# A fused attention and feed-forward kernel: table loads and filler products as operations of their own, in a new written-out order

## The chip, the cores and the metric

The kernel runs on one core of one Trainium2 chip. The metric is the device time of one execution in microseconds. Five engines work beside each other, each through its own queue in order: PE (TensorE, matrix products), ACT (ScalarE, table functions and scaling), DVE (VectorE), POOL (GpSimd) and SP (SyncE, which here only issues DMA).

## The reference, cut to what matters

```python
# q, k, v: (4, 8, 768, 64), proj: (64, 6); w_in: (512, 2048), w_out: (2048, 512)
q_bits = (np.einsum('bhsd,dk->bhsk', q, proj) > 0)       # the same for k
q_bucket = np.sum(q_bits * 2 ** np.arange(6), axis=-1)
mask = q_bucket[:, :, :, None] == k_bucket[:, :, None, :]
scores = np.where(mask, q @ k.T / 8, -1e9)
attn = softmax(scores)                                   # over the last axis, + 1e-9
x = (attn @ v).transpose(0, 2, 1, 3).reshape(3072, 512)
h = x @ w_in
out = (h * tanh(softplus(h))) @ w_out                    # Mish
```

Attention is allowed only between a query and a key whose six sign bits agree; the result, of 3072 rows, goes through a feed-forward block with the Mish function.

## The kernel before

The work is cut into units of 256 query rows (two chunks of 128) over all eight heads: 12 units, three to each of the four batches. A unit has eight **slots** of attention (four pairs of heads, two chunks), numbered n = 0 to 95 over the kernel, and eight **groups** m of the feed-forward block (256 of the 2048 inner columns each), 0 to 95 as well, which run some slots behind.

Most fp32 values are carried as the sum of two fp16 numbers (hi and lo), so that PE can work in fp16: each long product is three fp16 products. Unit 0 is the exception: its probabilities are transposed on PE in fp32 and its products are fp32, since the weights have not been split yet.

A slot n is made of these operations, named as in the code: `S{n}` scores on PE (L878), `max` over the keys on DVE (L884), `scl` two or four small DVE or POOL instructions that make the scale and bias of the exponential (L890 to L896), `exp` two on ACT (L909), `sums` and `rv` (L922 to L931) the reciprocal of the row sums. In unit 0, `tp32` transposes the probabilities on PE (L950) and `tc32` copies them back (L955); later units form `hi` and `lo` (L374, L375, L390) and transpose through DMA (`ptturn`). `V{p}` is the product with V (L992, L999). `H{m}` is the first feed-forward product (L1044 to L1050), `mish` its function on ACT (L1066), `g_hi` and `g_lo` its split, `O{m}` the second product (L1095 to L1101).

Unit 0 carries one-time work as well: the K, Q and V of the first batch are scaled by the size of their squares (`square` on ACT or `gram` on PE, L438, with `trace` on DVE, L440, then `st` on PE, L457 and L458, `half` and `pw`), split (`k_hi`, `k_lo`, ...), transposed (`tp` on PE, L414, `tc`, or through DMA) and hashed (`hp` on PE, L712, `hsum` and `bits` on DVE, L716 and L720). The weights are converted (`w_u`, `w_sign` L543, `w_low` L556 or L559, `w_join` L563) and later split (`w_hi`, `w_lo`).

ACT holds one table of functions at a time. Exp and Mish are in different tables; scaling, copying and squaring are in both. Before the change the loads (ACT_TABLE_LOAD) are placed by the compiler ahead of the first function that needs the other table.

**What sets the order.** Every operation is recorded by `op(name, alternatives, reads, writes)`, with one alternative for each engine that could do it and a cost in ns. `ORDER` is a table of numbers, worked out ahead by a planner that is not part of the file: it gives the operations in the order in which they are issued, a letter behind a number picking the second, third or fourth alternative (another engine). So each engine's queue, and which engine does a step, follow from this table. The functions that the change touches are `gram`, `att_front`, `att_exp` and `ffn_mish`.

Of the kernel before, what the change touches and what calls it, by code (L numbers as in the profile page):

```python
# [14 lines left out]
AF = mybir.ActivationFunctionType  # L15
# [3 lines left out]
P = 128  # L19
# [68 lines left out]
37 88 14 22 7 0 3 1 2 23 24 25 63 73 38c 6 8 9 13 10 15 152 5 4 40 41 18 19 42 74 11b 12 20 21 26c 53b 75 76 77b 43 28  # L88
39b 29 66 16 44 55 30 45 27c 46 47 48 307 54 31 32 65 78 34 79 49 33 35 36b 67 83 84 213 214 215 89 90b 50 62 51 56 52
80 81 82 114b 91 168 169 85 86 113 87 153b 104 108 109 110b 17 92 93 94 123 57 58 59 60 115c 154b 95 96 97 170 99 98  # L90
100 111 105 112 132 101 102 155 69 70 162c 116 64 133 171 124b 172 61 103 135 136 68 256 257 258 129d 130 137 117 134
147 156 173b 148 149 138 139 140 141 72 107 131 118 119 120 106 121 144 145 150 163b 175 157 151 158 159 160 142 146
71 205b 164 165 464 185 125c 186 188 189 190 174b 126 143b 211 212 206b 207 216b 122 187 200 201 176 167 177 178 180
202 166 191 192 197 198 308 309 372 378 193b 373 374 179 208 458 459 460 194 182d 183 199 225 203 379 128 380 184 127
204 226 248 375 227 222 223 249b 250c 251 254 230b 161 231 376c 229 228 310b 224 240 241 242 232c 233 243 244 245 311b
247 195 268 269 270 246 219c 305 271 209 265 272 196b 210 273 217 253 274b 266 255 461b 236d 237 238 262d 263 465 181
283 284 234 220 275 286 276 267 279c 285 259b 287 221 239 466 235 260 370 293c 292 294 295b 264 252 299 280 281 277
288 289 291 261 290 313c 300 301b 278 326b 462b 296 297 218b 282b 314 306 315 371 321 322 323c 324 312 327 328b 317
325 298 318 316c 432 434 329 330 344d 302 303 352 467 433 456 319 320 345 353 354 304 332b 333 435 347c 346 348 349
463 483 350 351 355 457 484 356 391 334c 335 336 337 468b 357 383b 384 385 441 485 486 392 393 338c 394 387 487 488  # L100
# [103 lines left out]
KV0 = (-1, -0.5, 0, 2)  # L204
WAT = (0, 2, 4, 5, 6, 7, 8, 8, 9, 9, 9, 11, 11, 11, 11, 11)
Q_AT = 2
SECOND = (1, 3, 5, 7)
QPE, KPE = 4, 2
KV_GRAM, Q_GRAM = 4, 2
LAG = 3  # L210


def BACKBONE(NA, NM):


    for blk in range(NA // 4 + LAG):
# [1038 lines left out]
```

## Time and profile before

| what | value |
|---|---|
| median of 3 runs | 843.06 us (841.53 to 843.43) |
| the profiled execution, its own time | 841.4 us |
| its span from first to last instruction | 839.6 us |
| PE busy | 794.9 us (95%) |
| DVE busy | 714.6 us (85%) |
| ACT busy | 632.1 us (75%), of which 92 table loads |
| POOL busy | 93.6 us (11%) |
| table loads ahead of Exp, ahead of Mish | 45 of 1283 ns, 46 of 1283 ns |

The profiled execution is 1.66 us under the median. The shares are means over very different stages: the first 182 us hold unit 0 and the one-time work, and PE, DVE and ACT take turns; after that PE is busy nearly without a break. An instruction's idle time is the time in which its engine had nothing else to do before it, and the releaser is what ended that. "PEclk" is the share of the full clock that TensorE was granted; half of it is 1.2 GHz.

### The profile page before, as it was taken

What the parts mean: (1) busy time and instruction counts of PE and PEld (TensorE: products, weight loads), DVE (VectorE), ACT (ScalarE), POOL (GpSimd) and SP (SyncE); (2) the same over time, 40 slices, a digit from 0 to 9 for tenths busy, and PEclk for the clock granted to TensorE, in tenths of its full rate; (3) what the DMA queues carried; (4) which work ended last, traced back from release to release, by engine and by line L of the source; (5) the groups of instructions that cost most, each with busy time, mean ns of one, the idle gap of its engine ahead of it and who ended that gap; (6) DMA issues with size and microseconds to landing.
All of it is one profiled execution on the core that took longest, in us unless ns stands there. A gap on an engine that the chain in (4) does not pass through costs nothing. (4 is left out here: it accounts for less than half of the span.)

```text
span 839.6 us, 16631 instructions
## 1 busy us (share of the span) xinstructions
PE 794.9 (95%) x6508; PEld 546.2 (65%) x6508; DVE 714.6 (85%) x1334; ACT 632.1 (75%) x972; POOL 93.6 (11%) x96
## 2 busy tenths in 40 slices
PE   4788989789999999999999999999999999999997
PEld 4656556466668578578577586577577577576664
DVE  6798999898989888989998998899999889888522
ACT  6777889987798687689878688679888688587410
POOL 5445424322230000000000000000000000000000
PEclk9899999999999999999999999999999999999999
DMA  9985878769999869899989987899997848655700
GB/s 281 197 253 178 215 179 195 120 147 186 203 181 181 165 120 158 175 171 180 185 170 175 159 176 154 142 171 196 201 157 159 168 96 160 123 95 102 157 1 26
DMA packets 400303, 135.58 MB, mean 161 GB/s; under 512 B 370528, under 2 KB 391008, under 8 KB 400224
## 3 DMA queue, kind: packets, MB, share of 16 engines
q1 hardware_dynamic: 400224, 134.52, 80.3%
q8 instruction: 51, 0.84, 0.4%
q14 instruction: 28, 0.23, 0.1%
HBM read 35.65 MB, written 6.29 MB: 50 GB/s over the span
## 5 line engine op out<-in xcount | busy, mean ns | idle before, releaser
L909 ACT ACTIVATE pb<-ps_s,svb 128x768 f32<-128x768 f32 x192 | 188.7, 986 | 58.6 <-DVE svb L896 50.6
L1048 PE MATMUL ps_acc<-X,wi 128*128 128x256 f16 x704 | 191.9, 273 | 0.8 <-ACT ffb L1066 0.8
L1050 PE MATMUL ps_acc<-X,wi 128*128 128x256 f16 x704 | 191.8, 273 | 0.0
L1049 PE MATMUL ps_acc<-X,wi 128*128 128x256 f16 x704 | 191.8, 272 | 0.0
L884 DVE TENSOR_REDUCE svb<-ps_s 128x2 f32<-128x1536 f32 x96 | 168.2, 1752 | 14.7 <-PE ps_s L878 11.1
L390 DVE SCALAR_TENSOR_TENSOR hl<-pb,svb,hl 128x768 f16<-128x768 f32 x172 | 174.5, 1022 | 6.5 <-ACT hl L374 4.0
L878 PE MATMUL ps_s<-KT,QT 128*128 128x512 f16 (+1 forms) x768 | 141.8, 328 | 6.3 <-ACT pb L909 5.3
L1099 PE MATMUL ps_o<-wo,ffb 128*128 128x512 f16 x352 | 133.4, 379 | 0.0
L1101 PE MATMUL ps_o<-wo,ffb 128*128 128x512 f16 x352 | 133.4, 379 | 0.0
L1100 PE MATMUL ps_o<-wo,ffb 128*128 128x512 f16 x352 | 133.4, 379 | 0.0
L878 PEld LDWEIGHTS <-QT 128*128 128x128 f16 x768 | 73.3, 98 | 56.6 <-issue 14.5
L374 ACT ACTIVATE hl<-pb,svb 128x768 f16<-128x768 f32 x80 | 73.4, 930 | 35.0 <-DMA PT<-hl 21.4
L992 PE MATMUL ps_t<-PT,VT 128*64 128x256 f16 x1584 | 94.6, 274 | 3.0 <-DMA PT<-hl 2.3
L1066 ACT ACTIVATE ffb<-ps_acc,smalls 128x512 f32<-128x512 f32 x88 | 59.3, 684 | 48.0 <-PE ps_acc L1050 46.9
L992 PEld LDWEIGHTS <-VT 128*64 128x64 f16 x1584 | 83.8, 110 | 17.3 <-issue 16.8
L1049 PEld LDWEIGHTS <-wi 128*128 128x128 f16 x704 | 68.8, 98 | 12.9 <-issue 1.8
L1048 PEld LDWEIGHTS <-wi 128*128 128x128 f16 x704 | 68.8, 98 | 11.6 <-issue 1.6
L1050 PEld LDWEIGHTS <-wi 128*128 128x128 f16 x704 | 68.8, 98 | 8.3 <-issue 0.2
L390 DVE SCALAR_TENSOR_TENSOR ffb<-ffb,smalls 128x512 f16<-128x512 f32 x88 | 65.2, 747 | 3.4 <-ACT ffb L374 0.9
L909 ACT ACT_TABLE_LOAD x45 | 57.7, 1283 | 12.1 <-DVE svb L896 4.7
L1101 PEld LDWEIGHTS <-ffb 128*128 128x128 f16 x352 | 34.4, 98 | 41.5
L1066 ACT ACT_TABLE_LOAD x46 | 59.0, 1283 | 0.8
(212 smaller groups left out, 991.9 us busy)
## 6 DMA issues: line engine op xcount, KB each, us to landing
out_dram<-ffb SPq DMA_DIRECT2D x24, 256.0 KB, 2.8
stg<-in_q_dram SPq DMA_DIRECT2D x10, 512.0 KB, 4.8
stg<-in_k_dram SPq DMA_DIRECT2D x12, 384.0 KB, 3.9
stg<-in_v_dram SPq DMA_DIRECT2D x12, 384.0 KB, 3.6
wo<-in_moe_w_out_dram SPq DMA_DIRECT2D x7, 512.0 KB, 4.9
stg<-in_moe_w_out_dram SPq DMA_DIRECT2D x7, 512.0 KB, 4.4
stg<-in_moe_w_in_dram SPq DMA_DIRECT2D x6, 512.0 KB, 4.5
wi<-in_moe_w_in_dram SPq DMA_DIRECT2D x6, 512.0 KB, 4.5
```

What stands on the lines that cost most here:

```text
L390: return [("DVE", 215 + 1.035 * n, port(lambda: nc.vector.scalar_tensor_tensor(out=dst, in0=src, scalar=sc, in1=hi, op0=ALU.mult, op1=ALU. ...
L878: nc.tensor.matmul(sc[:, hh * S + c0 * P:hh * S + c1 * P], QTb[:, u % 2, sl, qi], KTb[:, j, sl, hh * NCH + c0:hh * NCH + c1].rearrange("p ...
L884: op("max", [("DVE", 1790, lambda: nc.vector.tensor_reduce(out=sv[:, 0], in_=sc.rearrange("p (h e) -> p h e", h=2), axis=AX.X, op=ALU.max, ...
L909: EXP[n, hh] = op("exp", [("ACT", 1075, lambda hh=hh, t=t: nc.scalar.activation(pb[:, t], sc[:, hh * S:(hh + 1) * S], AF.Exp, bias=sv[:, 2 ...
L992: nc.tensor.matmul(pv[hh * D:(hh + 1) * D, 0:256], vt[:, w, hh * NCH + c], pt[:, hh, a * NCH + c].rearrange("p s t -> p (s t)"), start=(x ...
L1048: nc.tensor.matmul(o, wh, X[:, 0, c], start=(c == 0), stop=False)
L1049: nc.tensor.matmul(o, wh, X[:, 1, c], start=False, stop=False)
L1050: nc.tensor.matmul(o, wl, X[:, 0, c], start=False, stop=(c == NCC - 1))
L1066: op("mish", [("ACT", 690, lambda: nc.scalar.activation(ffb[:, t], PS[psn], AF.Mish, scale=h))], [psn] + ([(hsn, g, g + 1)] if u else []), ...
L1099: nc.tensor.matmul(PS[f"o{s}"], gh, hi[:, e], start=first, stop=False)
L1100: nc.tensor.matmul(PS[f"o{s}"], gh, lo[:, e], start=False, stop=False)
L1101: nc.tensor.matmul(PS[f"o{s}"], gl, hi[:, e], start=False, stop=last)
```

## The change

Three things are added as operations, and `ORDER` is a new table from a planner in which two rules of waiting were corrected (the planner's text is not part of the kernel).

- `fill`: ahead of each of the eight slots of unit 0, four operations that each issue eight 128x128x128 products of ones into an unused part of the PSUM bank `ps_g`; each has an empty alternative. The new table takes 10 of the 32: two ahead of the first PE operation, two behind the first two `st`, two among the first transposes, two between the scores of slots 0 and 1, and two behind the scores of slot 2. The other 22 are empty.
- `pre_e` and `pre_m`: ahead of each pair of `exp` and each `mish`, an operation that loads the table, with an empty alternative. The new table takes 12 of 96 and 7 of 96. Where none is taken, the compiler still places its own load. The program then has 94 loads besides the first one (before: 91); one of the 7 is followed by a second load of the same table.
- `gram` had two places in `ps_g`, used in turn; it now has one, since `fill` takes the second.

```diff
@@ the first and the last line of the table @@
-37 88 14 22 7 0 3 1 2 23 24 25 63 73 38c 6 8 9 13 10 15 152 5 4 40 41 18 19 42 74 11b 12 20 21 26c 53b 75 76 77b 43 28
...
+2967 2968 2961c 2962 2969 2914 2911 2970b 2971b 2972 2973 2974b 2975b 2976
@@ above BACKBONE @@
+NFILL = 4
@@ gram @@
-        i = 2 * half + gram_n[half] % 2
-        gram_n[half] += 1
+        i = 0
@@ att_front @@
+        if u == 0:
+            for _ in range(NFILL):
+                def busy():
+                    for _ in range(8):
+                        nc.tensor.matmul(ps_g[:, P:2 * P], ones, ones, start=True, stop=True)
+                BANK.append(op("fill", [("PE", 427, busy), ("PE", 0, lambda: None)], ["ones"]))
         op(f"S{n}", [("PE", 1300, pe)], [(f"QT{u % 2}.{x}", 4 * j, 4 * j + 4) for x in range(2)] +
@@ att_exp @@
+        op("pre_e", [("ACT", 1290, lambda: nc.scalar.preload_act_table(AF.Exp)), ("ACT", 0, lambda: None)])
@@ ffn_mish @@
+        op("pre_m", [("ACT", 1290, lambda: nc.scalar.preload_act_table(AF.Mish)), ("ACT", 0, lambda: None)])
```

Where the new table leads differs from the old one from the start to about the place that PE reached at 373 us before, DVE at 387 us and ACT at 384 us; behind that the queues of PE, DVE and ACT hold the same operations in the same order. Line numbers of the changed file are 11 to 19 higher: L884 is L901, L720 is L731, L1066 is L1085.

On PE, the first `gram` now stands behind the first transposes (it stood between the first two `st`); the second keeps its place among the hashes ahead of the last transposes of the K of slot 0, but the load that it reads (K of the third pair of heads) is issued seventh and no longer ninth; the third stands behind those transposes (it stood among them), ahead of the last `st` and of S0; and the fourth behind S0. On SP the first weights' load goes from the eighth place to the fifteenth.

The queue of DVE behind the maximum of slot 0 (svb holds the softmax numbers of a slot, hsum and hsum_k the sums of the hash, tok_65 and PT take the hash bits, ps_g is the bank of `gram`). Before:

```order
L884 TENSOR_REDUCE svb<-ps_s 128x2
L890 TENSOR_SCALAR svb<-svb,smalls 128x1 x2
L894 TENSOR_SCALAR svb<-svb 128x1 x2
L716 TENSOR_REDUCE hsum<-ps_t 128x72
L720 TENSOR_SCALAR tok_65<-hsum 128x12x6 x2
L384 COPY PT<-PT 128x12x64
L716 TENSOR_REDUCE hsum_k<-ps_t 128x72
L720 TENSOR_SCALAR PT<-hsum_k 128x12x6 x2
L850 TENSOR_SCALAR smalls<-smalls 128x1
```

After:

```order
L901 TENSOR_REDUCE svb<-ps_s 128x2
L451 SCALAR_TENSOR_TENSOR ps_g,smalls<-ps_g,ffb 128x128
L727 TENSOR_REDUCE hsum<-ps_t 128x72
L731 TENSOR_SCALAR tok_65<-hsum 128x12x6
L861 TENSOR_SCALAR smalls<-smalls 128x1
L727 TENSOR_REDUCE hsum_k<-ps_t 128x72
L731 TENSOR_SCALAR PT<-hsum_k 128x12x6 x2
L861 TENSOR_SCALAR smalls<-smalls 128x1
L472 TENSOR_SCALAR smalls<-ps_t 128x1
L396 COPY wo<-wo 128x12x64
L731 TENSOR_SCALAR tok_65<-hsum 128x12x6
```

The four instructions of the scale of slot 0 (L890, L894) are gone from DVE, `trace` has come in, and the first of the two bits of tok_65 and the bits of hsum_k stand ahead of the second.

POOL at the same place (L548 is `w_sign`, L925 `sums`, L372 a hi part; in the changed file L559, L943, L384). Before:

```order
L372 TENSOR_SCALAR stg<-stg 128x1024
L381 TENSOR_SCALAR wo<-wo 128x12x64
L548 TENSOR_SCALAR wi<-stg 128x1024
L925 TENSOR_SCALAR svb<-svb 128x2
L548 TENSOR_SCALAR wo<-wo 128x1024
L552 TENSOR_SCALAR wo<-wo 128x1024
```

After:

```order
L384 TENSOR_SCALAR wo<-wo,smalls 128x12x64
L907 TENSOR_SCALAR svb<-svb,smalls 128x2
L913 TENSOR_TENSOR svb<-svb 128x2
L384 TENSOR_SCALAR PT<-X,smalls 128x12x64
L457 TENSOR_SCALAR smalls<-smalls 128x1
L820 TENSOR_SCALAR smalls<-smalls 128x1
L559 TENSOR_SCALAR wo<-wo 128x1024
L943 TENSOR_SCALAR svb<-svb 128x2
```

The scale of slot 0 (L907, L913) is now on POOL between two hi parts of K, and the `w_sign` that stood ahead of the sums has moved back. In the same way the scales of slots 11, 13 and 14 and, later, 19 have come to POOL; slot 9's has gone from it to DVE.

ACT around the Mish of group 5 (wi and wo are weights being split or converted, tok_64 takes the hi part of Q). Before:

```order
L424 ACTIVATE wo,smalls<-wo 128x1024
L1066 ACT_TABLE_LOAD
L1066 ACTIVATE ffb<-ps_acc_820 128x512
L374 ACTIVATE tok_64<-X,smalls 128x16x64
L424 ACTIVATE wi,smalls<-wi 128x1024
L909 ACT_TABLE_LOAD
L909 ACTIVATE pb,svb<-ps_s,svb 128x768
```

After:

```order
L386 ACTIVATE wo<-wo,smalls 128x1024
L1084 ACT_TABLE_LOAD
L567 ACTIVATE wo<-wo 128x512
L436 ACTIVATE wo,smalls<-wo 128x1024
L1085 ACTIVATE ffb<-ps_acc_896 128x512
L386 ACTIVATE tok_64<-X,smalls 128x16x64
L924 ACT_TABLE_LOAD
L927 ACTIVATE pb,svb<-ps_s,svb 128x768 x2
```

The load for Mish (L1084, an operation of its own) stands two steps ahead of the function, and the load for Exp (L924) stays right ahead of it.

## Rows read from the trace of the kernel before

**Rows 1.** Windows by stage: busy us (instructions) of each engine, granted clock, DMA share, GB/s.

```profile
0.00:42.00 42.00, 27.10 (x260) 22.14 (x262) 29.20 (x82) 29.70 (x45) 21.57 (x27) 0.92 0.94 239
42.00:182.00 140.00, 118.49 (x765) 78.37 (x760) 130.82 (x224) 120.31 (x177) 52.23 (x50) 0.98 0.74 182
182.00:347.00 165.00, 164.53 (x1408) 114.00 (x1408) 146.70 (x280) 132.08 (x207) 19.82 (x20) 1.00 0.94 174
347.00:780.00 433.00, 429.42 (x3680) 295.91 (x3679) 387.98 (x718) 337.28 (x526) 0.00 (x0) 1.00 0.85 157
```

**Rows 2.** Groups by line within 42 to 182 us: busy, mean ns, idle before.

```profile
L1066 ACT ACT_TABLE_LOAD x6 | 7.7, 1283 | 0.1
L909 ACT ACT_TABLE_LOAD x5 | 6.4, 1283 | 1.2 <-DVE svb L896 1.0
L1066 ACT ACTIVATE ffb<-ps_acc 128x512 f32<-128x512 f32 x8 | 4.7, 593 | 0.1
```

**Rows 3.** The windows view on four short stretches, columns as in rows 1.

```profile
23.41:26.82 3.41, 3.41 (x24) 3.35 (x23) 2.59 (x6) 1.67 (x3) 2.77 (x2) 0.50 1.09 195
33.65:37.06 3.41, 3.41 (x28) 3.03 (x27) 2.56 (x11) 2.86 (x5) 0.00 (x0) 0.50 1.04 136
74.61:78.02 3.41, 3.41 (x11) 2.46 (x10) 2.77 (x6) 3.41 (x4) 0.00 (x0) 0.50 0.66 221
166.77:170.18 3.41, 3.15 (x18) 1.28 (x17) 3.41 (x4) 2.71 (x6) 0.39 (x1) 0.50 0.40 80
```

**Rows 4.** Timeline of PE: start, us, instruction, count, idle before and releaser.

```profile
13.09 0.82 PE L438 MATMUL ps_g<-X 128*128 128x128 bf16 x6 [0.17 <-DMA X<-in_k_dram]
13.71 0.84 PE L414 MATMUL ps_s<-unit,PT 128*128 128x128 f16 x6
14.80 0.85 PE L438 MATMUL ps_g<-wo 128*128 128x128 bf16 x6
16.89 0.48 PE L878 MATMUL ps_s<-KT,QT 128*128 128x512 f16 x2
```

**Rows 5.** Timeline of DVE behind the maximum of slot 0.

```profile
20.18 0.34 DVE L890 TENSOR_SCALAR svb<-svb,smalls 128x1 f32<-128x1 f32 x2
21.06 1.25 DVE L720 TENSOR_SCALAR tok<-hsum 128x72 f16<-128x72 f32 x2
22.83 0.30 DVE L720 TENSOR_SCALAR PT<-hsum_k 128x72 f16<-128x72 f32 x2
```

**Rows 6.** Timeline of PE: transposes at both clocks.

```profile
19.90 0.49 PE L414 MATMUL ps_s<-unit,PT 128*128 128x128 f16 x6 [1.22 <-ACT KT L416]
23.78 1.49 PE L950 MATMUL ps_s<-ffb,pb 128*128 128x128 f32 x6
33.51 2.73 PE L950 MATMUL ps_s<-ffb,pb 128*128 128x128 f32 x12 [2.25 <-ACT pb L909]
37.10 1.53 PE L950 MATMUL ps_s<-ffb,pb 128*128 128x128 f32 x12
```

**Rows 7.** Timeline ahead of the scores of slot 5: PE, then DVE.

```profile
48.09 0.18 PE L457 MATMUL ps_t<-smalls,ones 128*128 128x1 bf16 x1 [1.64 <-DVE smalls L461]
...
46.37 1.40 DVE L890 TENSOR_SCALAR svb<-svb,smalls 128x2 f32<-128x2 f32 x1
```

**Rows 8.** Timeline of POOL: two softmax scales that it worked out.

```profile
78.17 1.51 POOL L890 TENSOR_SCALAR svb<-svb,smalls 128x2 f32<-128x2 f32 x1 [6.28 <-DVE svb L884]
79.77 0.82 POOL L896 TENSOR_TENSOR svb<-svb 128x2 f32<-128x2 f32 x1
165.77 0.31 POOL L890 TENSOR_SCALAR svb<-svb,smalls 128x2 f32<-128x2 f32 x1 [0.84 <-DVE hw L461]
```

**Rows 9.** Groups by line and shape of DVE within 42 to 182 us.

```profile
L559 DVE TENSOR_SCALAR wo<-stg 128x1024 uint16<-128x1024 uint16 x3 | 2.3, 756 | 0.0
L375 DVE TENSOR_SCALAR hl<-pb,svb 128x768 f16<-128x768 f32 x8 | 5.4, 679 | 0.5 <-DVE svb L931 0.3
L390 DVE SCALAR_TENSOR_TENSOR wi<-wi,smalls 128x1024 f16<-128x1024 f32 x7 | 8.9, 1277 | 0.0
```

More of the change, by code (lines that the diff above doesn't have):

```diff
@@ L87 @@
 ORDER = """
-37 88 14 22 7 0 3 1 2 23 24 25 63 73 38c 6 8 9 13 10 15 152 5 4 40 41 18 19 42 74 11b 12 20 21 26c 53b 75 76 77b 43 28
[L89 to L97, printed above, removed]
@@ new lines @@
+731b 986 1009 1045 910 911 987 988 990 979 991 1012b 1013 950 1040 966 1042 912 913 978 1014c 1023 1016 1043c 1044
+1047 855 727 1024 1056 904 1021 980 1077 1078 981 785b 1026b 1048b 1049 1094 1017 1093 905 1025b 958 982 1058 1059b
+1060 1015c 906 902 908 1022 1102 993 1239 994 1061 1018 1240 1019 1027 1028 1029c 1030 995 907 909 996 997b 936 914
+1063 1032c 1035 870b 1031c 1050 1051 941 1052 1054 1130 815b 1135 1036 891b 1033 1034 1010c 1055 999 1193 1069 1070
+1132 1071 1137 1064c 1079 1065 1080 937 1133b 1081 1053 1073 1000 1084 1072c 1066 1134 1074 1241 1075 1083 1076 1103
@@ new lines @@
+1645 1646 1721b 1722 1723c 1724 1701 1667 1668 1657 1659 1638 1660 1658 1617 1725 1758 1757 1582c 1726b 1727 1741
+1728b 1669b 1670 1661 1729 1585 1586 1588 1587 1589 1671 1692c 1693 1920 1694c 1673 1703 1704 1674 1675 1705 1742b
+1743 1696 1744c 1736 1737b 1738 1773 1695c 1739c 1676 1677c 1679 1774 1708 1706b 1707 1709 1697 1710 1712 1810 1811b
+1812 1813b 1662 1711 1740 1680 1730 1698 1782 1731 1732b 1713 1733b 1734 1715 1699 1716 1827 1594 1681 1682 1678c 1684
+1683 1735 1749c 1714 1814 1815 1816b 1817 1873 1820 1750 1818b 1745 1828b 1829 1759 1760 1761 1762b 1763 1685 1809
@@ new lines @@
+2335b 2599 2336 2337c 2325 2326 2405 2401b 2402 2262c 2370b 2403c 2404 2398 2438 2347 2348 2339 2340 2265 2406b 2407
+2408b 2409 2338c 2341 2342 2349b 2350 2266 2268 2416 2351 2372c 2373 2267 2269 2454 2383 2374c 2384 2353 2354 2355
+2356 2421 2385 2375 2378 2379 2417b 2418 2357c 2419c 2376 2377 2359 2422b 2423 2424c 2382 2420 2386b 2387 2388 2426
+2317b 2318 2389c 2390 2391 2495 2410 2411 2412 2392 2437 2413b 2414 2393 2395 2415 2553 2429c 2394 2274 2427 2496b
+2497 2453 2498b 2490 2491b 2492 2493b 2430 2431c 2433 2439 2440 2441 2444 2396 2432c 2435 2462 2512 2507 2442b 2443
@@ new lines @@
+2665 2565 2653 2715b 2716 2701 2663 2712c 2713 2661b 2662 2668b 2669 2654 2670c 2629 2671 2672 2666 2677 2678 2679
+2680b 2681 2746 2691 2731 2717c 2630 2566 2667 2747 2674 2682 2683c 2684 2685 2703 2755 2673 2686c 2748 2689 2687 2704
+2705 2706b 2707 2708 2722c 2719 2675 2690 2718 2767 2720 2721 2732 2688 2756 2757 2723 2725 2724c 2784 2733 2734b
+2735b 2736 2758 2726 2737 2738b 2787 2788b 2789 2749 2739 2740c 2742 2728 2792 2768 2803 2727 2793b 2794 2750 2751
+2741c 2744 2790c 2752b 2753 2754 2791 2785b 2729 2808 2743 2770 2759 2760 2804b 2805 2761c 2763 2806b 2825 2762 2771
```

204 lines of the change are left out of this document (102 added, 102 removed).

## The prediction

> **What bounds the kernel now.** I read the windows by stage first [rows 1]. From 182 to 780 us PE has work at nearly every moment: it is idle 0.47 us of 165 and 3.58 of 433, while DVE and ACT have slack (DVE busy 89% and 90%). There only less work for PE would help, and the change gives it none. From 42 to 182 us it is DVE: 130.82 of 140 us busy (93%), against 86% for ACT and some 85% for PE. The first 42 us belong to nobody: DVE 29.20, ACT 29.70, PE 27.10 busy, all in chains of short steps that wait for each other. So what the change wins, it wins ahead of 182 us, and there in two ways: a shorter chain at the start, or less time on DVE between 42 and 182 us. Whatever is won there moves the whole PE-bound rest forward by as much.
>
> The second view is the clock [rows 3]. Four stretches of 3.41 us ran at 0.50, that is 1.2 GHz, and PE was busy in nearly all of each. What came before them: PE had only short products between slot 0's scores and 23 us, and had waited 2.25 us ahead of 33.51 us for ACT [rows 6]. Ahead of 16.6 us the record of the clock is missing, but the pace tells it: six transposes take 0.84 us at 13.71 us [rows 4] and 0.49 us at 19.90 us [rows 6].
>
> **The start, to the scores of slot 0 (16.89 us).** Before, the second `gram` waits for its load until 13.09 us and holds the transposes behind it for 0.62 us (to 13.71 us); the third stands among them at 14.80 us and is as long [rows 4]. After, the load comes two places earlier. At 239 GB/s [rows 1] two loads of 393 kB are 3.3 us, so the first wait goes, and the third `gram` is out of the way. That is 2 x 0.62 = 1.2 us. Against it, S0 now stands behind an `st` that needs the third `gram`'s trace on DVE: I take 0.5 us back. If the six fillers ahead of 13 us bring the clock up by then, two groups of transposes on the chain take 0.49 for 0.84 us: 0.7 us more. Bounds 0.7 and 1.4; I take 1.1, since the fillers are on PE while it has nothing else. Each filler is eight products of 128 columns, 1.1 us at the pace of the row at 13.09 us (0.82 us for six); should one end late, it delays the next `st` by under that.
>
> **From the scores of slot 0 to those of slot 1.** Here DVE goes from the end of the maximum (20.18 us) to the bits of hsum_k (23.13 us): the scale, a pair of bits of 1.25 us, a copy and the bits [rows 5]. After, the scale is on POOL and the slow bit is behind, and the same chain is a trace, two reductions and three short bits, some 1.6 us. But the transposes of the probabilities need both exponentials, which need the scale, and these set the start: about 0.5 us is won. The pace gives more. At half clock six transposes of L950 take 1.49 us at 23.78 us, and twelve take 2.73; at full clock twelve take 1.53 [rows 6], so 1.2 us are lost for twelve. Two fillers stand here. The copies between the transposes on ACT hold part of it back: I take 1.3 of 1.7 for both together; bounds 0.4 (clock stays down) and 1.7.
>
> **Slots 1 to 3.** Two fillers stand in the wait ahead of 33.51 us. If they hold the clock, the twelve transposes there win their 1.2 us [rows 6]; if not, nothing. I take 1.2, because the stretch with 3.41 us at 0.50 began within that very wait. **Ahead of slot 5** PE waits 1.64 us for a `half` behind a scale that takes 1.40 us on DVE [rows 7]. One of the two `half` now stands ahead of that scale, the other still behind it; bounds 0 and 1.2, taken 0.4.
>
> The start then gives 1.1 + 1.3 + 1.2 + 0.4 = 4.0 us (bounds 1.5 and 5.5). DVE has to be able to follow: it is idle 12.8 us of the first 42 [rows 1], part of them before the first load has landed, so there is room for 4.0 us, if not for much more.
>
> **DVE from 42 to 182 us.** I counted DVE's queue up to the scale of slot 18, on which the first Mish of unit 1 and with it the PE-bound part hang. 36 operations leave it and 31 come. Most pair off. Net, three `w_low` (0.756 us) and three `hi` (0.679 us) leave [rows 9], with three scales, four sums and two other small ones of 0.15 to 0.8 us: some 7 us. Three `w_u`, two `v_hi`, two copies and a bit of the same lengths come, and a `w_lo` (1.277 us) and a `v_lo`: some 6.5 us. That is 0.5 us in favour, to which I give bounds of 0 and 2.
>
> **What moves to POOL.** The scales of slots 0, 11, 13 and 14 are now POOL's. The exponentials wait for them, and behind these ACT's whole queue. POOL took 2.42 us for the scale at 78.17 us; at 165.77 us its first instruction took 0.31 in place of 1.51 us, some 0.6 us for the whole [rows 8], and DVE takes some 0.5 (0.34 us for the first half of the scale of slot 0 [rows 5]). So the price is 0.1 to 1.9 us each; on the three later ones, where the exponential is not always what DVE waits for, I take 1.0 us in all.
>
> By the Trainium skill ("SBUF — State Buffer", "Reading the diagram") POOL and DVE share a pair of ports as an exclusive lock for a whole instruction, and the loser blocks. The trace agrees in kind: the first instruction took five times as long at one place as at the other; by the rule alone the dear price would hold for all four scales.
>
> **The table loads.** In 42 to 182 us there are 11 [rows 2]; the time ACT stood idle ahead of them is 0.1 + 1.2 us, all that an early load can hide there, and the changed order has as many loads in that stretch. The function behind a load had almost no wait of its own (0.1 us for eight). I take 0; bounds 0 and 1.2. The three loads more (3 x 1.283 = 3.8 us) lie behind 182 us mostly, where ACT is busy 80% [rows 1] and PE covers them; without that cover they would cost those 3.8 us.
>
> The Trainium skill ("ScalarE: Activation LUTs", "What ACT_TABLE_LOAD costs") puts a drain of about 1380 ns on top of every 1283 ns load. The trace shows no such gap: 0.1 us ahead of eight Mish. By that rule the three loads would cost ACT 8 us, still under PE's cover.
>
> **The rest.** The half-speed stretches at 74.61 and 166.77 us have no filler and stay. Behind 182 us only few steps change places on PE, and its sequence ends alike; 0, with 1 us to either side.
>
> Sum: 4.0 + 0.5 - 1.0 = 3.5 us. On the profiled execution 841.4 becomes 837.9 us; the median stands 1.66 above it, so 843.06 - 3.5 = 839.6 us.
>
> **The rivals.** (1) *DVE too gets free.* Its idle 9.2 us between 42 and 182 us [rows 1] shrink by 3 with the new order, and the start gives its upper bound: 5.5 + 2 + 1.2 = 8.7 at most, 7 in the middle: 836.0 us. For it: the order was drawn anew for all engines. Against it: a queue that is 93% full has little left. (2) *The start's gain is waited off.* DVE takes its work at the same times as before because it is fed by loads and by POOL; then 4.0 us of earlier scores only lengthen the waits ahead of DVE: no change, 843 us within 1. For it: DMA runs at 0.94 of its engines in the first 42 us [rows 1], so the loads that feed the conversions come no earlier. Against it: DVE's idle time at the start is waiting for PE and ACT in the rows that I read. The fillers not raising the clock is the weak form of this: 1.5 + 0.5 - 1.0 = 1.0, 842 us. (3) *POOL's scales are dear: slower.* If the scales of slots 0, 11, 13 and 14 all take 2.42 us, each holds its exponentials 1.9 us longer: 7.6 us, in place of the 1.0 taken. Net 7.6 - 4.5 = 3.1 us slower, 846.2 us. It decides from the third dear one on: two cost 3.8 and leave a gain of 0.7. For it: a scale in the saturated stretch was the dear one. Against it: a late exponential costs only when DVE has nothing else queued, and its queue is full there.
>
> **How the numbers follow.** The measurement can tell 0.2%, 1.7 us: faster is below 841.4, slower above 844.7. Chances: forecast 0.47 (837.5 to 841.3), rival 1 0.15, rival 2 0.21, rival 3 0.17. Faster has 0.47 + 0.15 = 0.62; same 0.21; and slower 0.17. The range reaches from the upper bound of the gain, 843.06 - 8.7 = 834.4, to the rival on the other side, 846.2; within it I leave out a tenth at either end: 834.5 to 846.0.
>
> **What the profile of the changed kernel would show.** The clock at 1.00 in the windows around 24 and 34 us; S0 at about 15.8 us, the `st` ahead of the scores of slot 5 near 44.1 in place of 48.09 us; DVE still over 90% busy to the start of the PE-bound part, and that start (the first H of unit 1 behind two Mish) near 178.5 us in place of 182. Wrong would be: the stretches at 0.50 still there in spite of the fillers; scales on POOL of over 2 us with ACT waiting behind them; or slot 5 early and the PE-bound part not.

## The result, and the profile after

The changed kernel takes **834.07 us** (median of 4 runs, 831.96 to 834.33), against 842.29 us for the kernel before on the same chip (4 runs, 840.37 to 843.43): a ratio of 0.9899, with a 95% interval of 0.9873 to 0.9925, or 8.5 us less by the ratio. The forecast was 3.5 us less. The profiled execution took 834.31 us, its span is 832.5 us.

Three landmarks are used from here on: the start of the scores of slot 5; the "first H", which is the first H of unit 1 that has to wait for a Mish (the third of that unit), where the PE-bound part starts; and the time from the scores of slot 20 to the last PE instruction. Before they are 48.61, 181.91 and 643.4 us, after 44.74, 170.75 and 647.7 us. So 3.9 us are won up to slot 5, 7.3 us more up to the first H, and 4.4 us are given back in the part of which I had said that nothing changes.

The windows by stage, after, as in [rows 1] (the limits moved with the landmarks; columns: stretch, its length, busy us and instructions of PE, PEld, DVE, ACT and POOL, granted clock, DMA share, GB/s):

```profile
0.00:42.00 42.00, 31.99 (x371) 25.05 (x372) 31.34 (x85) 31.86 (x52) 21.03 (x32) 1.00 0.99 256
42.00:170.80 128.80, 114.25 (x733) 76.74 (x731) 121.39 (x217) 115.67 (x169) 46.56 (x54) 0.96 0.83 193
170.80:336.20 165.40, 164.80 (x1408) 113.65 (x1408) 145.43 (x268) 138.81 (x215) 9.92 (x12) 1.00 0.91 174
336.20:772.00 435.80, 429.94 (x3678) 295.10 (x3677) 387.87 (x717) 336.99 (x522) 0.00 (x0) 1.00 0.84 156
```

The second stage is 11.2 us shorter, and DVE is still busy 94% of it; but ACT, which had 86%, now has 90%. Between the maximum of slot 5 and the scale of slot 18 the same view gives, first for before, then for after:

```profile
52.41:177.28 124.87, 106.06 (x653) 69.42 (x650) 116.49 (x181) 107.71 (x156) 49.24 (x45) 0.97 0.74 180
...
48.55:166.12 117.57, 104.30 (x647) 68.99 (x644) 112.85 (x178) 106.88 (x156) 43.48 (x49) 0.96 0.83 189
```

DVE works 3.6 us less and is idle 4.7 in place of 8.4 us; ACT does the same work and is idle 10.7 in place of 17.2 us. Less of the idle time is waiting of these two for each other: by the views of waits of the same stretches DVE waits 3.4 us for ACT before and 0.4 after, and ACT waits 9.6 us for a softmax scale ahead of its exponentials before and some 4.3 after. The longest of these waits, first before, then after:

```profile
DVE wi L563 <- ACT wi L556: 1.9, 1, 1.9
ACT pb L909 <- DVE svb L896: 6.3, 5, 2.7
ACT pb L909 <- POOL svb L896: 2.3, 1, 2.3
...
DVE wi L574 <- ACT wi L567: 0.4, 1, 0.4
ACT pb L927 <- DVE svb L913: 1.9, 4, 0.8
ACT pb L927 <- DVE svb L911: 1.4, 2, 0.7
ACT pb L927 <- POOL svb L913: 1.0, 1, 1.0
```

The clock, as in [rows 3]: in this execution full where the fillers stand, half at a new place (109 us) and for 6.83 us around the scores of slot 18 (160.97 us), where it was half for 3.41 us before (166.77 us, slot 18 at 169.26).

```profile
23.41:26.82 3.41, 2.28 (x17) 1.42 (x16) 2.17 (x3) 3.41 (x4) 1.41 (x2) 1.00 1.19 140
33.65:37.06 3.41, 3.41 (x29) 2.33 (x29) 3.00 (x3) 3.39 (x6) 1.46 (x2) 1.00 1.01 204
109.32:112.73 3.41, 3.41 (x9) 1.53 (x7) 3.41 (x4) 3.38 (x5) 0.71 (x2) 0.50 0.90 269
157.10:163.93 6.83, 3.46 (x25) 2.01 (x22) 6.19 (x13) 6.80 (x13) 2.23 (x4) 0.50 0.67 150
```

### The profile page after: what moved, and what is told of

The parts are those of the page before. It is cut to its first block, busy times and chain, and to the rows that moved or that the text cites. A ratio compares the mean times of both kernels' runs of the same rounds, so it can differ in the third digit from the quotient of the medians.

```text
span 832.5 us, 16767 instructions
## 1 busy us (share of the span) xinstructions
PE 797.2 (96%) x6588; PEld 546.7 (66%) x6588; DVE 706.5 (85%) x1320; ACT 635.9 (76%) x976; POOL 77.5 (9%) x97
## 5 line engine op out<-in xcount | busy, mean ns | idle before, releaser
L927 ACT ACTIVATE pb<-ps_s,svb 128x768 f32<-128x768 f32 x192 | 188.6, 986 | 49.6 <-DVE svb L913 43.1
L1066 PE MATMUL ps_acc<-X,wi 128*128 128x256 f16 x704 | 192.1, 273 | 0.2 <-ACT ffb L1085 0.2
L901 DVE TENSOR_REDUCE svb<-ps_s 128x2 f32<-128x1536 f32 x96 | 168.2, 1752 | 19.7 <-PE ps_s L889 15.8
L402 DVE SCALAR_TENSOR_TENSOR hl<-pb,svb,hl 128x768 f16<-128x768 f32 x174 | 176.5, 1022 | 5.6 <-ACT hl L386 3.2
L1085 ACT ACTIVATE ffb<-ps_acc,smalls 128x512 f32<-128x512 f32 x88 | 59.0, 684 | 47.7 <-PE ps_acc L1068 45.6
L1066 PEld LDWEIGHTS <-wi 128*128 128x128 f16 x704 | 68.7, 98 | 11.7 <-issue 1.8
L1120 PEld LDWEIGHTS <-ffb 128*128 128x128 f16 x352 | 34.3, 97 | 42.3 <-DVE ffb L402 0.9
L1119 PEld LDWEIGHTS <-ffb 128*128 128x128 f16 x352 | 34.3, 98 | 37.3
L387 DVE TENSOR_SCALAR hl<-pb,svb 128x768 f16<-128x768 f32 x89 | 54.9, 617 | 3.1 <-DMA PT<-hl 1.4
```

The lines of the kernel that those rows point to most:

```text
L402: return [("DVE", 215 + 1.035 * n, port(lambda: nc.vector.scalar_tensor_tensor(out=dst, in0=src, scalar=sc, in1=hi, op0=ALU.mult, op1=ALU. ...
L901: op("max", [("DVE", 1790, lambda: nc.vector.tensor_reduce(out=sv[:, 0], in_=sc.rearrange("p (h e) -> p h e", h=2), axis=AX.X, op=ALU.max, ...
L927: EXP[n, hh] = op("exp", [("ACT", 1075, lambda hh=hh, t=t: nc.scalar.activation(pb[:, t], sc[:, hh * S:(hh + 1) * S], AF.Exp, bias=sv[:, 2 ...
L1066: nc.tensor.matmul(o, wh, X[:, 0, c], start=(c == 0), stop=False)
L1119: nc.tensor.matmul(PS[f"o{s}"], gh, lo[:, e], start=False, stop=False)
L1120: nc.tensor.matmul(PS[f"o{s}"], gl, hi[:, e], start=False, stop=last)
```

## The experiments

"Ratio" is against the kernel before on the same chip; a change of 0.001 is 0.84 us, and where two ratios are compared the difference is uncertain by some 2 to 3 us. Landmarks are from each kernel's one profiled execution, which can lie some us from the median.

| kernel | ratio (95%) | slot 5 | first H | slot 20 to last PE |
|---|---|---|---|---|
| before | 1 | 48.6 | 181.9 | 643.4 |
| changed | 0.9899 (0.9873, 0.9925) | 44.7 | 170.8 | 647.7 |
| after_again | 0.9898 (0.9876, 0.9921) | 46.6 | 171.2 | 647.4 |
| a_402 | 0.9959 (0.9944, 0.9973) | 46.0 | 176.0 | 646.7 |
| a_scl9 | 0.9920 (0.9898, 0.9943) | 44.7 | 173.1 | 647.5 |
| b_402 | 1.0021 (1.0003, 1.0038) | 48.6 | 182.0 | 645.4 |
| b_scl9 | 0.9997 (0.9985, 1.0009) | 48.9 | 183.1 | 643.7 |
| b_9_402 | 0.9996 (0.9984, 1.0008) | 47.4 | 181.3 | 643.4 |
| a_nofill | 0.9911 (0.9883, 0.9940) | 46.3 | 170.8 | 643.0 |
| a_nofill2 | 0.9915 (0.9894, 0.9936) | 47.3 | 174.9 | 642.3 |
| b_fill | 1.0051 (1.0035, 1.0067) | 47.3 | 181.2 | 647.9 |
| b_pad80 | 1.0051 (1.0033, 1.0070) | 49.2 | 180.5 | 647.9 |
| a_pad128 | 0.9849 (0.9827, 0.9871) | 46.1 | 171.4 | 642.9 |
| ab_s5p | 0.9959 (0.9943, 0.9974) | 45.5 | 178.0 | 643.1 |
| ab_s13p | 0.9910 (0.9883, 0.9936) | 43.4 | 172.9 | 644.9 |
| ba_s5 | 0.9933 (0.9911, 0.9955) | 49.6 | 179.9 | 642.7 |
| ba_s13 | 1.0058 (1.0037, 1.0079) | 49.1 | 186.1 | 641.1 |
| ba_s13b | 1.0002 (0.9984, 1.0019) | 46.7 | 180.9 | 642.1 |
| a_nopre_p | 0.9900 (0.9882, 0.9917) | 45.0 | 170.8 | 645.4 |
| a_scldve_p | 0.9912 (0.9891, 0.9932) | 48.0 | 177.0 | 643.5 |

### Single pieces that left ACT and POOL for DVE

Between slots 9 and 14, I took two pieces that the new order has on DVE for links of the chain that led to the first H before: the scale of slot 9 (2.42 us on POOL [rows 8]) and the seventh weights piece, whose low part took 2.49 us on ACT and whose sign part 2.48 us on POOL, with ACT idle until it ended (timelines of the kernel before):

```profile
107.28 2.49 ACT L556 ACTIVATE wi<-wi 128x1024 int16<-128x1024 uint16 x1
109.86 2.48 POOL L548 TENSOR_SCALAR wi<-wi 128x1024 bf16<-128x1024 int16 x1 [11.81 <-ACT wi L556]
112.38 1.16 ACT L374 ACTIVATE wi<-wi 128x1024 f32<-128x1024 f32 x1 [2.61 <-POOL wi L548]
```

After, the two parts stand on DVE at 1.33 and 1.31 us:

```profile
94.78 1.33 DVE L570 TENSOR_SCALAR wi<-wi 128x1024 uint16<-128x1024 uint16 x1
96.15 1.31 DVE L554 TENSOR_SCALAR wi<-wi 128x1024 int16<-128x1024 int16 x1
```

I put them back, one at a time, in the new table, and ran the changed kernel itself beside it:

```diff
-446c 447
+446b 447b
-364
+364c
```

The first pair of lines is a_402, the second a_scl9.

> The changed kernel once more, as the mark for the runs beside it: about 834 us, 8 us under the kernel before. The start of the PE-bound part (H11) is expected near 171 us as in its first profile; the place where the rest of the gain is given back, between slot 48 and the end (H11 came 11.2 us earlier than before, the last product 6.8 us), is expected to move by a us or two between profiles if it is chance, and to be the same again if it belongs to the order.

> The changed kernel with two letters put back: the low part of the seventh piece of the weights on ACT and its sign part on POOL, as before the change (2.49 and 2.48 us there, 1.3 us each on DVE now). If the detour over ACT and POOL was a link of the chain, H11 comes 2 to 4 us later and the whole takes 836 to 838 us. If the path is DVE's work alone, taking 2.6 us of work from DVE makes it up to 2.6 us faster, 831.5 to 834 us.

> The changed kernel with one letter of the table put back: the scale of slot 9 on POOL, as before the change. If that choice was worth what the rows of before say (2.41 us on POOL against 0.42 on DVE, on the chain to slot 10), H11 comes 1.5 to 2 us later and the whole takes 836 us. If DVE's full queue hides it (the rival), 834 us within 0.7.

The weights piece cost 0.6% in ratio and 5.2 us at the first H, slot 9's scale 2.4 us at the first H, though its ratio lies within the interval of the changed kernel's. So far it looked as if two links that I had not priced held most of the gain. The opposite trial on the old table:

```diff
-402b 403b
+402c 403
-323c
+323
```

The first pair alone is b_402, the second alone b_scl9, both are b_9_402.

> The kernel before with one edit of the table: the low and the sign part of the seventh weights piece, which it has on ACT (2.49 us) and then on POOL (2.48 us), both on DVE, as the changed kernel has them; their places in the order stay. Theory 1, the detour over ACT and POOL was a link of the chain of before by itself: the first H of unit 1 starts about 4 to 5 us earlier than 181.9 us and the time is near 838 us. Theory 2, the detour costs only in the new order, where all else is early: the first H moves by under 1.5 us and the time is 841.5 to 843.5 us. Theory 3, DVE was the bound of before in this stretch, and two more instructions there (0.75 to 1.3 us each) make it slower: 844 to 845 us.

> The kernel before with the scale of slot 9 on DVE in place of POOL (2.41 us there), as in the changed kernel, and nothing else. Theory 1, this scale stood on the chain: the scores of slot 12 and the first H of unit 1 come 1.5 to 2.5 us earlier, near 840.3 us. Theory 2, the time behind it is made up by waits on something else (the weights detour behind it): the first H moves by under 0.7 us and the time is that of before, 842 to 843 us.

> The kernel before with both edits, the scale of slot 9 and the two parts of the seventh weights piece on DVE. If the two are links of one chain in a row, their gains add: what the two single kernels give together, near 835 to 836 us, and that is nearly all of what the changed kernel gives (834.1). If they stand on two chains beside each other, the pair gives more than the sum. If DVE becomes the bound, it gives no more than the weights pieces alone, near 838 us.

All three of my first theories fell: in the old order neither piece is worth anything, nor are both, and the weights piece alone costs 0.2%. In the trace of b_9_402 DVE is idle 1.0 us between 59 and 111 us, in place of 3.4 before, and ACT 5.6 us between 98 and 122 us, in place of 2.9. That fits two limits side by side in the old order, where work taken from one only fills the other; the traces do not prove it. What a piece costs when it is put back into the new order is therefore not what it had given.

### Where the gain lies: the two orders cut and joined

At the scores of slot 5 the two orders have nearly the same operations behind them (eleven stand on the other side), at those of slot 13 too (eight). So the first part of one can be joined to the rest of the other. The parts with the new start carry 48 short products more (the reason is in the next section), those with the old start have no fillers.

In ab_s5p and ab_s13p the table is edited like this, in ba_s5, ba_s13 and ba_s13b with the two orders exchanged:

```diff
 the new order up to and with S5 (or S13)
-the rest of the new order
+all other operations, in the order of before
```

> The new order with its fillers up to the scores of slot 5, the 48 short products ahead of them, and from there on the order of before. PE's code blocks lie as in the kernel before. Theory 1, the early start is carried, as the prediction has it: slot 5 near 46 us (the 48 products cost up to 1.3 of the 3.9 us), the first H of unit 1 2.5 us earlier than before, 179.4 us, and 838.5 to 839.5 us. Theory 2, it is waited off in the old order: the first H within 0.7 us of 181.9 and 841 to 842 us. Theory 3, the seam costs, as it did with the parts the other way round (4.5 us between slots 5 and 8 there): 184 us and later, 844 us or more.

> The new order with its fillers up to the scores of slot 13, the 48 short products ahead of them, and from there on the order of before (five and three operations stand on the other side of the cut). Theory 1, what the new order wins ahead of slot 13 is carried by the old order too, as the start's 3.9 us were: slot 13 near 109.9 us, the first H of unit 1 some 65.3 us behind it, near 175.2, and 833 to 835 us. Theory 2, the old order behind slot 13 has no room for it (its DVE and ACT wait on each other between 98 and 122 us): the first H at 178 us or later, no better than with the cut at slot 5, 837 us or more.

> The order of before up to the scores of slot 5, without fillers, and the new order from there on (four operations stand ahead of the cut that the new order has behind it, and seven the other way). Theory 1, the gains of the stretches add, as the prediction has it: slot 5 as before (48.6 us), the first H of unit 1 near 174.6 us, 7.3 earlier than before, and 835 us. Theory 2, the start does not matter, the new order behind slot 5 is all of the gain: the first H near 171 us, as in the changed kernel, and since PE's code blocks lie as before, 831 us. Theory 3, the two parts only work together: 177 us and later, 838 us and more.

> The order of before up to the scores of slot 13, without fillers, and the new order from there on (three and five operations stand on the other side of the cut). Theory 1, gains add by stretch: the scores of slot 13 as before (116.6 us), the first H of unit 1 near 178.7 us, 3.2 earlier than before (what the new order wins behind slot 13), and 839 us. Theory 2, everything ahead of slot 14 is waited off: near 171 us and 831 us. Theory 3, the later part only pays for what the earlier one has prepared: 181 to 182 us and 842 us.

> The order of before up to the scores of slot 13, without fillers, and the new order behind it, as in the run with that cut, but with the two early table loads that the new order has ahead of slot 13 empty (there they stood behind the cut and loaded tables for nothing: slots 13 to 14 took 17.0 us, in place of 11.4 before). Theory 1, gains add by stretch: slot 13 near 116.7 us, the first H of unit 1 near 178.5 us, 3.4 earlier than before, and 837 to 839 us. Theory 2, the later part only pays for what the earlier one prepared: the first H at 181 to 182 us and 841 us.

From the new start on, each part adds a gain: with the start alone 0.9959 (3.4 us), with the order up to slot 13 0.9910 (4.1 us more), with all of it 0.9849 (a_pad128 below, 5.1 us more). The first H follows at first, from 181.91 to 177.98 and 172.93 us; the last part moves it only 1.6 us more, to 171.36 us, and 2.0 us of its gain lie behind slot 20 in the profiled executions (644.9 to 642.9). To this part belong 17 of the 19 early table loads. So theory 1 held for ab_s5p: the old order carries the early start to the end.

The other way round the gain is smaller. ba_s5 wins 5.6 us where 9.2 were left, a difference of 3.6 that is uncertain by some 3 us. In its profiled execution, the longest of its six, slots 5 to 8 take 4.4 us longer than before; from slot 9 to the first H it takes 101.8 us, like the new order (102.2) and not like the old one (107.9). In ba_s13 two early table loads of the new order fell behind the cut, where they load for nothing (a fault of the edit; 1.0058). Without them ba_s13b wins nothing: the new order wants O of group 4 on PE ahead of slot 14, and ACT, still holding two of the long low parts, comes to the Mish that it needs 4.2 us behind the scores of slot 13 (119.25 us), in a_pad128 1.2 us behind them (111.06 us). So the last part pays only for what the earlier ones have prepared.

### The fillers, and where PE's code is loaded

The fillers emptied, in a_nofill and, later, once more in a_nofill2:

```diff
-                    for _ in range(8):
+                    for _ in range(0):
```

> The changed kernel with its fill operations left empty (the table is the same, the products of ones are not issued). Theory 1 (the fillers give what the clock gives): the granted clock falls to 0.5 again around 24 and 34 us, the scores of slot 5 come 2.5 to 3.5 us later than 44.7 us, and the whole takes 2.5 to 3.5 us longer, near 837 us. Theory 2 (the new order alone made the start shorter, the fillers only fill): slot 5 within 1 us, the whole within 1 us of 834. Theory 3 (the fillers also bring the later gain, by way of the clock at slots 9 and 10): 5 us and more longer, 839 us or above.

The median was 1.4 us above the changed kernel's (1.0 by the ratio), within the intervals; but the profiled execution was the fastest of the six (829.63 us), and its last part took 643.0 us. On the old table, ten fillers at the same places:

```diff
+FILL = {23: 2, 41: 2, 43: 1, 45: 1, 96: 1, 100: 1, 131: 2}
+            for _ in range(FILL.get(n, 0)):
+                yield self.busy
```

> The kernel before with ten fillers of eight 128x128x128 products of ones at the places that the changed kernel gives them (two ahead of the first product, two behind the first two st, two among the first transposes, two between the scores of slots 0 and 1, two behind those of slot 2), and nothing else. Both theories: full clock near 24 and 34 us, and the scores of slot 5 come 2 to 3 us earlier. Theory 1, as the prediction has it, the early start is carried to the end: the first H of unit 1 is 2 to 3 us earlier and the time 839.5 to 840.5 us. Theory 2, the start is waited off between slots 9 and 14: the first H moves by under 0.7 us, 842 to 843 us.

Slower by 0.5%, which neither theory had. The clock was full to 42 us and slot 5 came 1.3 us earlier. By slot 9 0.6 of that were left, and they went when a stretch at half clock fell on its scores; the first H came 0.7 us earlier all the same. But from slot 20 on the kernel lost 4.5 us.

The fillers do not hold the clock in every execution. Of the ten traces without them, each has a stretch at half clock that starts between 22.8 and 34.0 us, and of the ten with them one; but six of these ten have one that starts between 14.4 and 15.8 us.

In the table, the last column is 646.7 to 647.9 us for each kernel with just 80 added products, and 641.1 to 645.4 us for all others, in the old order and in the new. What differs there is where transposing DMAs are long:

The changed kernel, from the view of DMA on 334.5 to 338.3 us, in which three transposes of probabilities are issued (packets, MB and share of 16 engines of each queue, then the issues with the median us to landing):

```profile
q1 hardware_dynamic: 1990, 0.50, 73.8%
q8 instruction: 1, 0.02, 1.5%
...
PT<-hl SPq DMA_TRANSPOSE x3, 5.2
```

The same three in a_pad128, below, at 333.9 to 338.0 us:

```profile
q1 hardware_dynamic: 2180, 0.55, 71.3%
...
PT<-hl SPq DMA_TRANSPOSE x3, 4.0
```

The queue q8, of the kind "instruction", moves blocks of 16 kB, 51 in a run: one for about 128 products with their weight loads, so I take it for PE's code. From all twenty traces I took those transposes of the probabilities, from 200 to 780 us, that start with no earlier DMA of the kernel under way: 552. Of these, 362 have no block in them, and take 3.63 to 3.92 us. All 36 that take over 5.2 us (5.31 to 6.54) have a block of q8 that starts 3.0 to 3.7 us behind their own start; 40 others with a block at that point are not long. Such long ones are three or four in each kernel with the fillers alone, two in b_pad80 below, and one or two in all others. From slot 20 on PE is idle 6.8 us in the changed kernel, and waits there for transposing DMAs:

```profile
PE ps_t L723 <- DMA KT<-tok: 1.9, 2, 1.3
PE ps_t L1010 <- DMA PT<-hl: 0.8, 2, 0.4
```

In a_pad128 below it is idle 3.6 us, and none of it is put down to a DMA. How much of the loss goes by these waits alone is open, since b_pad80 loses as much with fewer long transposes. 80 products more at the start shift all later blocks against the work. 128 more should shift them by a whole block, that is, not at all:

```diff
+PAD = (304, 48)
...
+            if n == PAD[0]:
+                yield self.pad
+        for _ in range(PAD[1]):
+            nc.tensor.matmul(ps_g[:, P:P + 1], ones, ones[:, 0:1], start=True, stop=True)
```

This is a_pad128, the new order with 80 + 48; b_pad80 is the old order without fillers and with PAD = (23, 80).

> The changed kernel with 48 more products of ones, of one column each, ahead of the first filler, where PE is idle; with the 80 of the fillers that makes 128 products more than without fillers. In the traces PE's program is loaded in blocks of 16 kB, one for about 128 products with their weight loads, and each transposing DMA of over 5.2 us in place of 3.8 has the start of such a block 3.0 to 3.7 us behind its own. Theory 1, what is given back behind 190 us (S20 to the end takes 647.4 us with fillers and 643.0 without) comes from where these blocks fall: 128 products are one whole block, so the blocks fall as without fillers, S20 to the end takes 643 to 644 us, and the time is near 830 us. Theory 2, it comes from the fillers themselves (the clock, or the memory that they write): 647 us and 834 us. Theory 3, it is scatter between runs: anything from 643 to 648.

> The kernel before with 80 products of ones, of one column each, ahead of its first product, where PE is idle, and nothing else. They are as many instructions as the ten fillers, but at one place and short. Theory 1, the place of PE's code blocks: S20 to the end takes 647 to 648 us, as with the fillers at their places, in place of 643.4, and the time is 845 to 846 us. Theory 2, the fillers' place, length or clock: 643.4 us and the time of before, 842 us.

Both came out as theory 1 has it: the last part took 642.9 us with 128, and 647.9 us with 80 short products in one place, where neither the clock nor the fillers' places are in play. The trace of a_pad128 has 52 blocks, one more, and behind the scores of slot 20 they start at 14.5, 27.5 and 43.6 us, as without fillers (14.3, 27.2 and 43.3 in a_nofill) and not as in the changed kernel (3.3, 20.5 and 37.0). a_pad128, at **828.31 us** (827.36 to 830.07), beats both kernels: 0.9849 of before. So the place of the code blocks takes some 4.2 us from the changed kernel (0.9899 less 0.9849).

Yet with the blocks in the same place, the kernel without fillers had a median of 835.4 and a_pad128 828.3:

> The changed kernel with its ten fillers empty, once more: PE's code blocks lie as in the kernel with 128 products more (S20 to the end 643 us in both), yet the median of its runs was 835.4 us and that of the other 828.3. Theory 1, the fillers are worth some 6 us in most executions, and the one profiled execution without them (829.6) was a lucky one: the median comes out at 834 to 837 us again, and where the profile shows a run of that length, it shows more stretches at half clock ahead of 180 us and a later first H of unit 1 (176 to 178 us). Theory 2, the fillers are worth nothing and the first set of runs was disturbed: 828 to 830.5 us.

It was theory 1: 833.8 us, first H at 174.9 us. What the trace of this run shows is between slots 5 and 8, 20.0 us in place of 17.4 in a_nofill and 17.8 in a_pad128. DVE's four conversions and POOL's (timeline):

```profile
51.73 1.22 DVE L574 SCALAR_TENSOR_TENSOR wi<-wo,wi 128x1024 int32<-128x1024 int32 x1
52.64 1.38 POOL L384 TENSOR_SCALAR wi<-wi 128x1024 f32<-128x1024 f32 x1 [2.85 <-DMA wi<-in_moe_w_out_dram]
52.86 1.78 DVE L554 TENSOR_SCALAR wo<-stg 128x1024 int16<-128x1024 int16 x1
54.09 1.75 POOL L559 TENSOR_SCALAR wo<-wi 128x1024 bf16<-128x1024 int16 x1
54.53 1.92 DVE L570 TENSOR_SCALAR wo<-stg 128x1024 uint16<-128x1024 uint16 x1
56.67 2.26 DVE L574 SCALAR_TENSOR_TENSOR wo<-stg,wo 128x1024 int32<-128x1024 int32 x1
```

and in a_pad128:

```profile
51.07 1.22 DVE L585 SCALAR_TENSOR_TENSOR wi<-wo,wi 128x1024 int32<-128x1024 int32 x1
52.20 0.75 DVE L565 TENSOR_SCALAR wo<-stg 128x1024 int16<-128x1024 int16 x1
52.85 0.75 DVE L581 TENSOR_SCALAR wo<-stg 128x1024 uint16<-128x1024 uint16 x1
53.82 1.20 DVE L585 SCALAR_TENSOR_TENSOR wo<-stg,wo 128x1024 int32<-128x1024 int32 x1
55.85 1.13 POOL L395 TENSOR_SCALAR wi<-wi 128x1024 f32<-128x1024 f32 x1 [6.15 <-DMA wi<-in_moe_w_out_dram]
```

POOL starts when its weights land. Where DVE is through by then, its four take 3.9 us; where it is 0.7 us later and the load 3.2 us earlier, 7.2 us. The same four are long in ba_s5. By the medians the fillers, together with the 48 short products, are worth some 5.4 us with the blocks held in place; that this meeting is what they avoid is not shown: in the other trace without fillers, a_nofill, POOL meets only the last of the four (1.87 us), as it does in the changed kernel with them (1.85 us). In the changed kernel as it stands the two cancel but for about 1 us (0.9899 with, 0.9911 and 0.9915 without fillers).

### The table loads and POOL's scales

Both kernels have the 48 short products, so they are compared with a_pad128. In a_nopre_p (and the same for Mish), then in a_scldve_p:

```diff
-lambda: nc.scalar.preload_act_table(AF.Exp)
+lambda: None
...
-114c 436c 521c 550c 730c
+114 436 521 550 730
```

> The changed kernel with the 48 short products ahead of the first filler (828.3 us so far) and with all 19 taken table loads empty, so that the compiler's loads alone are left, each right ahead of its function. Theory 1, as predicted the early loads are worth nothing: within 1 us, 827.5 to 829.5. Theory 2, they hide loads on ACT's chain: one load of 1.28 us and up to three of them, 829.6 to 832 us. Theory 3, the three loads more and the early switches cost: 825 to 827 us.

> The changed kernel with the 48 short products (828.3 us so far) and with the scales of slots 0, 11, 13, 14 and 19, which the change moved to POOL, back on DVE at the same places in the order. POOL took 0.57, 1.92, 1.08, 1.19 and 1.52 us for them, DVE takes 0.42. Theory 1, they are dear and on the chain: 2 to 4 us less, near 825 us. Theory 2, as in the prediction's price of 1.0 us: near 827.3. Theory 3, DVE is the bound there, and they spare it: 829 to 831 us.

Without the early loads the time was 832.79 us, 0.0051 or 4.3 us worse than a_pad128. The first H did not move (170.84 us); the loss lies behind it. In the profiled executions the part from slot 20 on is 2.5 us longer, and PE waits longer for exponentials there; first a_nopre_p, then a_pad128:

```profile
PE ps_s L900 <- ACT pb L938: 4.4, 9, 0.7
...
PE ps_s L900 <- ACT pb L938: 2.5, 5, 0.7
```

The old order has 643.1 to 645.4 us there with no early load and the blocks in place, so this gain is against the new order without the loads, and not against the kernel before. Table loads between 182 and 340 us, first a_nopre_p, then the changed kernel (busy, mean ns, idle before them and what ended it):

```profile
L1096 ACT ACT_TABLE_LOAD x11 | 14.1, 1283 | 0.2
L938 ACT ACT_TABLE_LOAD x11 | 14.1, 1283 | 9.9 <-DVE svb L924 8.7 <-DVE hl L413 0.8 <-DVE svb L912 0.3
```

```profile
L924 ACT ACT_TABLE_LOAD x7 | 9.0, 1283 | 0.1
L927 ACT ACT_TABLE_LOAD x4 | 5.1, 1283 | 0.7 <-DVE svb L913 0.7
```

The compiler's load stands with the exponential behind its wait for the scale: ACT is idle 9.9 us, and only then loads for 1.28. As an operation of its own the load runs in that wait. One instance, the exponential ahead of slot 37 in a_nopre_p and in a_pad128:

```profile
313.44 1.28 ACT L938 ACT_TABLE_LOAD   x1 [0.99 <-DVE svb L924]
314.74 0.99 ACT L938 ACTIVATE pb<-ps_s,svb 128x768 f32<-128x768 f32 x1
```

```profile
310.64 1.28 ACT L935 ACT_TABLE_LOAD   x1
311.94 0.99 ACT L938 ACTIVATE pb<-ps_s,svb 128x768 f32<-128x768 f32 x1
```

With the scales on DVE again the time was 833.80 us, 0.0063 or 5.3 us worse. So the scales on POOL help. Its trace, of the longest of its six executions, shows 1.9 us at slot 5 and 5.7 us at the first H, and 23.9 us at half clock ahead of it in place of 13.7; how much of this is DVE's longer queue and how much the clock is not settled.

## Why the prediction was wrong

The direction was right; the gain was 8.5 us and not 3.5, and the time lies just under the range. By the runs the sum is: start 3.4, from slot 5 to slot 13 4.1, behind it 5.1, and 4.2 given back by the code blocks, 8.4 together. Each of these is the difference of two neighbouring kernels, so the sum had to close, and each is uncertain by 2 to 3 us. The first H, expected near 178.5 us, came at 170.75.

- **The start, 4.0 us: right in size, only in part by the cause given.** Slot 5 came 3.87 us earlier; its parts were 0.83 (forecast 1.1), 1.84 (1.3), 1.34 (1.2) and -0.14 (0.4). The wait of 1.64 us ahead of slot 5 [rows 7] went, but another came, for the transposing DMA of Q (timeline of PE):

```profile
41.29 0.56 PE L723 MATMUL ps_t<-pj,QT 128*128 128x12 f16 x16 [1.22 <-DMA QT<-tok]
...
44.23 0.18 PE L468 MATMUL ps_t<-smalls,ones 128*128 128x1 bf16 x1
```

  Over the four kernels each with this start and with that of before (the first eight rows of the table), slot 5 comes at 45.5 and 48.4 us on the mean, 2.9 us apart. Without fillers the new order still had it at 46.3 and 47.3 us. So the order gave some 1.6 us and the fillers some 1.3, where the forecast gave the clock that they hold up 2.5 (4.0 against 1.5 in its weak form); that the total came near is partly luck. The lower bounds of the four terms also add up to 1.1 and not to 1.5 us. ab_s5p shows that the start is carried to the end, 3.4 us of it, also in the old order. Rival 2 fell with it.
- **"DVE from 42 to 182 us", 0.5 us with bounds 0 and 2: the step that failed.** I counted which operations leave DVE's queue and which come, at fixed durations, and took the difference. The runs show 7.3 us between slot 5 and the first H (11.2 less 3.9), and 6.6 us from ab_s5p to a_pad128, which have the same start (177.98 to 171.36); by the ratio all of the new order behind slot 5 is worth 9.2 us, with what lies behind the first H. The count itself was near: at the mean lengths of before, DVE's instructions from the maximum of slot 5 to the scale of slot 18 are 0.7 us less. But DVE is busy 3.6 us less there, since its instructions also took less long and overlapped more (the second one of a 128x2 scale took 0.30 us on the mean before, 0.16 after), and idle 3.7 us less, which no count of operations can see. I had named this as rival 1 (836.0 us, chance 0.15), with "a queue that is 93% full has little left" against it. But the 7% were 9.2 us [rows 1], and ACT, at 86% and waiting 9.6 us for scales, was tied to it. Why the order as a whole wins this idle time, and no piece of it alone does, is argued and not shown.
- **What moves to POOL, a cost of 1.0 us: wrong in sign.** The five scales took 0.57 to 1.92 us there, so the bounds of one held; but moved back they cost 5.3 us. I priced the scale's own length and not the place in DVE's queue that it leaves. Rival 3 fell.
- **Slot 9's scale and the seventh weights piece: no price given.** I saw the first go from POOL to DVE and left it out. In the new order the two are worth 2.4 and 5.2 us at the first H, in the old one nothing.
- **The table loads, 0 with bounds 0 and 1.2: wrong.** The price was read from 42 to 182 us [rows 2], and there they are indeed worth nothing. They pay behind it, 4.3 us by the ratio, where I had only counted three loads more and let PE cover them. This does not come on top of the 9.2 us but is part of it, as are the scales of slots 11 to 19 on POOL.
- **"The rest", 0 with 1 us to either side: wrong.** The fillers' 80 products moved PE's code blocks, and the part from slot 20 on took 4.4 us longer, with queues that are the same behind 387 us of before. The view of DMA of the kernel before does list the queue of the code, and I gave it no price:

```profile
q8 instruction: 51, 0.84, 0.4%
```

- **Half-speed stretches:** those near 24 and 34 us went, as forecast; the one at 74.61 us went as well, one came at 109 us, and the one around slot 18 stayed and got longer. The place of such a stretch differs between executions of one kernel (after_again has one at 15.3 us, in spite of the fillers, and none at 109), so no price should hang on one of them.

The failed terms have both signs, so the sum was nearer than its parts deserve.

## What to carry to other kernels

Where two engines are both near 90% busy, an order worked out as a whole can win their idle time on both, and pieces of it tried alone on the old order show nothing; compare orders by cutting and joining them at a point that both pass with nearly the same work done. Ask of an added instruction not only what it costs where it stands: it moves the engine's code, and all code loads behind it, against the DMAs; a few short instructions in an idle stretch can move them back. Write a table load ahead of the wait of its function where that function waits for another engine.

## What the runs showed of the hardware

- PE's code comes, by the count of blocks and products, in blocks of 16 kB through the DMA engines, some 15 us apart. A transposing DMA with the start of one 3.0 to 3.7 us behind its own took 5.3 to 6.5 us in 36 of 76 cases; without a block it took 3.6 to 3.9.
- Beside POOL, the first instruction of a DVE scale of 128x2 took 2.38 us in place of 0.23 (kernel before, 177.28 us), until POOL's instruction ended (changed kernel, timeline):

```profile
102.66 2.38 DVE L907 TENSOR_SCALAR svb<-svb,smalls 128x2 f32<-128x2 f32 x1
...
102.51 2.50 POOL L559 TENSOR_SCALAR wo<-wo 128x1024 bf16<-128x1024 int16 x1 [6.36 <-ACT wo L567]
```

  The Trainium skill ("SBUF — State Buffer", "Reading the diagram") has the lock of the shared ports last for a whole instruction; these rows agree (both end within 0.03 us).
- A conversion of 128x1024 sixteen-bit numbers in place took 2.49 us on ACT and 2.48 us on POOL, and 1.31 to 1.33 us on DVE.
